# Key maskings of segments 1 to 3 on VectorE or ScalarE instead of GpSimd, and a new order of work, in a memory-attention and gated-FFN kernel

## The chip, the cores and the metric

The kernel runs on one core of a Trainium2 chip. The metric is the device time of one execution in microseconds (us). A core has five engines with an in-order queue each: TensorE (PE, matmuls; its weight loads are shown as PEld), VectorE (DVE), ScalarE (ACT), GpSimd (POOL) and SyncE (SP, which issues most DMAs). They are synchronised by semaphores alone.

## The reference

For 2048 tokens of width 512 (bf16) the reference mixes two branches with a gate per token, `g * a + (1 - g) * b`, g = sigmoid(x . gate_w).

```python
# branch a: 4 segments of 512 tokens, 32 heads of 16 channels
for s in range(4):
    logits = qs @ ks.T * 16 ** -0.5 + causal mask
    a_dot  = softmax(logits) @ vs
    a_mem  = (phi(qs) @ M) / (phi(qs) @ z + 1e-6)      # phi(t) = t + 1 where t > 0, else exp(t)
    out_s  = sigmoid(beta) * a_mem + (1 - sigmoid(beta)) * a_dot
    M += phi(ks).T @ vs;  z += phi(ks).sum()
a = concat(out_s) @ wo
# branch b: F = 1792
b = (relu(x @ W_gate) * (x @ W_up)) @ W_down
```

## The kernel before

The work goes by segments of 512 tokens. For each segment there are: projections q, k, v (`proj`, matmuls at L788 and L786); attention in 18 visits (`att`); the memory part (`mu`, L831, and `nd`, L851 to L863); the FFN in 14 blocks of 128 hidden channels (`ffn`, L1038); and the output (`outp`: L1070 for wo, L1077 for W_down), scaled and evacuated at L1086 and L1087.

Heads are taken in four groups G of eight. Keys lie with channels on partitions, so that 32 partitions hold two heads. The **key masking** (L803 to L807, tile `kp`) makes two copies of each group's 128x512 keys, p = 0 and 1; each copy is multiplied by a per-partition 0/1 column of `pm`, which keeps one head of each pair. So there are 2 x 4 = 8 maskings in a segment, 32 in all. Those of segment 0 run on DVE, the other 24 on POOL. `kp` is a ring of five slots (`kslot`), so a masking waits for the quad group that read its slot last.

A **visit** is a "quad" group of matmuls (L908, 32-row tiles, reading `kp` and `qT`), then an exponential on ACT over 2048 columns (L924, PSUM to `E`), then causal masks of the diagonal blocks on POOL (`affine_select`, L930; one pair of 64- and 128-partition pieces for each diagonal block). When all visits of a head group are through, a **PV** group (L964, 64-row tiles; 16 such groups in all) multiplies the weights with the values, DVE transposes the result (L974), forms and scales the reciprocals (L983, L985), POOL divides (`adT`, L987; in the last segment DVE), and DVE transposes back and adds the memory part (L990 to L993). The phi of two head groups is an ACT exponential (L770) with two DVE pieces: max and add into `ttmp` (L771), minimum (L772). FFN blocks are evacuated by a relu on ACT or DVE (L1046, L1047) and a product on DVE (L1049).

**The order** is not written by hand. Every operation is added to a list with its reads and writes, one or more engines that may run it, and a time for each engine in ns. A list planner (`Sched.run`, `ready`, `_choose`, `place`) plays the five engines forward by those times: it takes the operation that can start first, ties going by the priority of its queue and by a small random jitter, and so fixes each engine's queue and its semaphore waits once and for all. Where an operation names two engines, the planner puts it on the one on which it starts first. The jitter and four further settings (`knob`) are drawn from a list of seeds, one for each 8 us of planned PE time. For an operation whose name stands in `PORT` (key maskings, phi pieces, `rdg`, `ad`, `oa` among them) the planner also books that DVE and POOL wait for each other. On the chip the order is kept and the times are what they are.

The line for the masking before; the ACT form `ka` is defined a line above and not used:

```python
evs.append(sc.add(Op(([("pool", km, 660)] if s else [("dve", km, 350)]), ..., name=f"kmask{s}_{G}_{p}")))
```

Of the kernel before, what the change touches and what calls it, by code (L numbers as in the profile page):

```python
# [9 lines left out]
ALU = mybir.AluOpType  # L10
# [27 lines left out]
ADP = 1  # L38
# [501 lines left out]
def build_kernel(nc, A_x, A_wq, A_wk, A_wv, A_wo, A_beta, W_g, W_u, W_d, gate_w, out):  # L540
    _, S, D = A_x.shape
    F = W_g.shape[1]
    assert D == 512 and S % 512 == 0 and F % 128 == 0
    NSEG, KT, NF, NT = S // 512, D // 128, F // 128, S // 128
    EPS, SCALE = 1e-6, 16 ** -0.5
    sc = Sched(seeds=(140892, 17502, 0, 0, 0, 833601, 583263, 51094, 0, 212245, 56886, 641769, 290654, 823150, 60678, 0, 364216, 4435, 795879, 905041, 409277, 519825, 941044, 25370, 612543, 696634, 0, 758283, 835103, 656834, 0,))
    T = {}
    with contextlib.ExitStack() as stack:
        for name, shape, dt in plan(S, D, F):
            T[name] = stack.enter_context(nc.sbuf_tensor(name, shape, dt))  # L550
        PS = stack.enter_context(nc.psum_tensor("ps", [128, 8, 512], F32))
        for st in sc.streams:
            sc.sem[st] = stack.enter_context(nc.semaphore(f"s_{st}"))
        program(sc, nc, T, PS, A_x, A_wq, A_wk, A_wv, A_wo, A_beta, W_g, W_u, W_d, gate_w, out, NSEG, KT, NF, NT, EPS, SCALE)
        with nc.Block() as block:
            sc.emit(block)
    return sc


def program(sc, nc, T, PS, A_x, A_wq, A_wk, A_wv, A_wo, A_beta, W_g, W_u, W_d, gate_w, out, NSEG, KT, NF, NT, EPS, SCALE):  # L560
# [13 lines left out]
    def dve(fn, occ, **k):  # L574
        return op("dve", fn, occ, **k)
# [190 lines left out]
    def phi(s, px, G, dst, dn, src, slot, rd, acts, sbs):  # L766
        d0 = G - 1 if px == "q" else (G - 1) % EKN
        xv, pv = src[:, slot:slot + 2, :], dst[:, d0:d0 + 2, :]
        wr = [f"{dn}{d0}", f"{dn}{d0 + 1}"]
        acts.append(act(lambda e: e.activation(pv, xv, ACT.Exp), t_act(1024, False), reads=rd, writes=wr, name=f"{px}exp{s}_{G}"))  # L770
        sbs.append((pool if TSP else dve)(lambda e: e.tensor_scalar(V.ttmp[:, :, :], xv, 0.0, 1.0, ALU.max, ALU.add), 1160 if TSP else 400, reads=rd, writes=["ttmp"], name=f"{px}ts{s}_{G}"))  # L771
        sbs.append(dve(lambda e: e.tensor_tensor(pv, pv, V.ttmp[:, :, :], ALU.min), 700, reads=wr + ["ttmp"], writes=wr, name=f"{px}phi{s}_{G}"))  # L772

    def proj(s):
        pes, evs, sbs, acts, sps = [], [], [], [], []
        tok = s % XR * 512

        def pj(w, col, name, wname, tokmajor=False):
            early = s == 0 and name == "q" and col < 3
            ep = Epoch("att" if early else "proj")  # L780
            step = 1 if early else 2
            for k0 in range(0, KT, step):
                def fn(e, k0=k0):
                    for kt in range(k0, k0 + step):
                        if tokmajor:
                            ins = e.matmul(A(ep)[:, :], lhsT=V.xT[:, kt, tok + col * 128:tok + (col + 1) * 128], rhs=w[:, kt, :], start=(kt == 0), stop=(kt == KT - 1))  # L786
                        else:
                            ins = e.matmul(A(ep)[:, :], lhsT=w[:, kt, col * 128:(col + 1) * 128], rhs=V.xT[:, kt, tok:tok + 512], start=(kt == 0), stop=(kt == KT - 1))  # L788
                    return ins
                pes.append(pe(fn, mm(512, step), reads=[f"{wname}{kt}" for kt in range(k0, k0 + step)] + (xt(s) if not early or k0 > 1 else [x for x in xt(s) if x not in ("xT0_3", "xT0_5")]), name=f"{name}{s}_{col}", ep=ep, role="w2" if k0 else "w"))  # L790
            return ep
        def cp(fn, **k):
            return sc.add(Op([("dve", lambda e: fn(e, e.tensor_copy), t_dve(512)), ("act", lambda e: fn(e, lambda d, x: e.activation(d, x, ACT.Copy)), t_act(512))], **k))
        for G in range(4):
            ep = pj(V.wq, G, "q", "wq")
            qs = qslot(s, G)
            evs.append(cp(lambda e, f, ep=ep, qs=qs: f(V.qT[:, qs, :], A(ep)[:, :]), writes=[f"qT{qs}"], name=f"qcp{s}_{G}", ep=ep, role="r"))
            if s > 0 and G % 2:
                phi(s, "q", G, V.phiq, "phiq", V.qT, qs - 1, [f"qT{qs - 1}", f"qT{qs}"], acts, sbs)
            ep = pj(V.wk, G, "k", "wk")  # L800
            evs.append(cp(lambda e, f, ep=ep, G=G: f(V.kT[:, G, :], A(ep)[:, :]), writes=[f"kT{G}"], name=f"kcp{s}_{G}", ep=ep, role="r"))
            ks = kslot(s, G)
            kv = V.kT[:, G, :].rearrange("q (c k) -> q c k", c=8)  # L803
            for p in range(2):
                km = lambda e, kv=kv, p=p, ks=ks: e.tensor_scalar(V.kp[:, ks, :, 64 * p:64 * p + 64], kv, V.pm[:, p:p + 1], None, ALU.mult)  # L805
                ka = lambda e, kv=kv, p=p, ks=ks: e.activation(V.kp[:, ks, :, 64 * p:64 * p + 64], kv, ACT.Copy, scale=V.pm[:, p:p + 1])
                evs.append(sc.add(Op(([("pool", km, 660)] if s else [("dve", km, 350)]), reads=[f"kT{G}", "pm"], writes=[f"kp{ks}_{p}"], name=f"kmask{s}_{G}_{p}")))  # L807
            if s < NSEG - 1 and G % 2:
                phi(s, "k", G, V.ek, "ek", V.kT, G - 1, [f"kT{G - 1}", f"kT{G}"], acts, sbs)
                for g in (G - 1, G):  # L810
                    sps.append(dma("sp", lambda e, g=g: e.dma_start_transpose(V.phik[:, :, g * 128:(g + 1) * 128], V.ek[:, g % EKN, :]), 1 << 17, occ=1280.0, reads=[f"ek{g % EKN}"], writes=[f"phik{g}"], name=f"kT2{s}_{g}"))
        for tt in range(4):
            ep = pj(V.wv, tt, "v", "wv", True)
            evs.append(cp(lambda e, f, ep=ep, tt=tt: f(V.vaug[:, s % 2, tt, :, 0:16], A(ep)[:, :].rearrange("q (h c) -> q h c", c=16)), writes=[f"va{s % 2}_{tt}"], name=f"vcp{s}_{tt}", ep=ep, role="r"))
        if s == 0:
            pes = [p for k in "qkv" for p in pes if p.name[0] == k]
            pes[:3 * KT] = [pes[h * KT + kt] for kt in range(KT) for h in range(3)]
        return pes, evs, sbs, acts, sps
# [25 lines left out]
    def nd(s):  # L844
        pes, ds, sps = [], [], []
        for i in range(4):
# [7 lines left out]
            def nv(ep):  # L854
# [4 lines left out]
            ds.append(dve(lambda e, i=i: e.reciprocal(V.rdm[:, 32 * i:32 * i + 32], V.rdm[:, 32 * i:32 * i + 32]), 345, reads=[f"rdm{i}"], writes=[f"rdm{i}"], name=f"ndr{s}_{i}"))  # L859
            ds.append(dve(lambda e, i=i, ep=ep, rd=rd: e.scalar_tensor_tensor(V.amem[:, i % 2, :].rearrange("q (h c) -> q h c", c=16), nv(ep)[:, :, 0:16], V.gexp[:, 4 * s + i:4 * s + i + 1],  # L860
                                                                             rd.unsqueeze(2).to_broadcast([128, 32, 16]), op0=ALU.mult, op1=ALU.mult),
                          t_dve(512), reads=[f"rdm{i}", f"gexp{s}"], writes=[f"amem{i % 2}"], name=f"ndm{s}_{i}", ep=ep, role="r"))
            sps.append(dma("sp", lambda e, i=i: e.dma_start_transpose(V.amemT[:, :, i * 128:(i + 1) * 128], V.amem[:, i % 2, :]), 1 << 17, occ=1280.0, reads=[f"amem{i % 2}"], writes=[f"amemT{i}"], name=f"aT{s}_{i}"))  # L863
        return pes, ds, sps

# [10 lines left out]
    def att(s, between):  # L876
# [57 lines left out]
        def flush():  # L934
# [47 lines left out]
            gv = V.rdg[:, 32 * (G % (TNN // 2)):32 * (G % (TNN // 2)) + 32].rearrange("q (p c) -> q p c", p=2)  # L982
            ds.append(dve(lambda e: e.reciprocal(rv, Tv[:, :, :, 16]), 345, reads=tn, writes=[f"rden{G % 2}"], name=f"rden{s}_{G}"))  # L983
            ge = V.gexpT[:, 16 * s:16 * s + 16].rearrange("q (a t) -> q t a", t=4).unsqueeze(1).to_broadcast([128, 2, 4, 4])
            ds.append(dve(lambda e: e.tensor_tensor(gv.rearrange("q p (t a) -> q p t a", a=4), rv.rearrange("q p (t a) -> q p t a", a=4), ge, ALU.mult), 215, reads=[f"rden{G % 2}"] + gexpT_r[s], writes=[f"rdg{G % 2}"], name=f"rdg{s}_{G}"))  # L985
            av = V.adT[:, :].rearrange("q (c p e) -> q p c e", p=2, e=16)
            ds.append((dve if s == NSEG - 1 or not ADP else pool)(lambda e: e.tensor_tensor(av, Tv[:, :, :, 0:16], gv.unsqueeze(3).to_broadcast([128, 2, 16, 16]), ALU.mult), 690 if s == NSEG - 1 or not ADP else 1360, reads=tn + [f"rdg{G % 2}"], writes=["adT"], name=f"ad{s}_{G}"))  # L987
            os_ = (s * 4 + G) % OTN
            if s == 0:
                ds.append(dve(lambda e: e.transpose(V.oT[:, os_, :], V.adT[:, :]), t_dve(512), reads=["adT"], writes=[f"oT{os_}"], name=f"bt{s}_{G}"))  # L990
            else:
                ds.append(dve(lambda e: e.transpose(V.oTt[:, :], V.adT[:, :]), t_dve(512), reads=["adT"], writes=["oTt"], name=f"bt{s}_{G}"))
                ds.append(dve(lambda e: e.tensor_tensor(V.oT[:, os_, :], V.oTt[:, :], V.amemT[:, G, :], ALU.add), 435, reads=["oTt"] + [f"amemT{i}" for i in range(4)], writes=[f"oT{os_}"], name=f"oa{s}_{G}"))  # L993
            return pair

        at = {}
# [201 lines left out]
```

## Time and profile before

| | |
|---|---|
| median of 3 runs | 268.11 us (268.04 to 268.27) |
| the profiled execution | 268.02 us, span 266.3 us |
| granted TensorE clock | 1.000 |
| busy: PE, DVE, ACT, POOL | 259.5, 179.1, 176.8, 164.3 us |
| POOL: causal masks L930, key maskings L805, divide L987 | 256 x 435, 24 x 1565, 12 x 1082 ns |
| DVE: L771, L772, L860, L992, L985 | 615, 743, 747, 705, 259 ns (means) |
| ACT: exponentials L924 | 72 x 1875 ns |

The span is the time from the first to the last instruction of the program; the execution holds a little more. A group's line reads: source line, engine, operation, output tile <- input tiles, shapes, count | busy us, mean ns of one | idle time of the engine just before them, and what ended it. A row of the waits reads: who waited <- for whom: us in all, times, longest. A row of the timeline reads: start and length in us, engine, line, operation, count of merged instructions [idle before <- what ended it]; lengths of merged rows include gaps between their instructions. Matmuls are pipelined: one of 512 columns shows 380 ns, while the next starts 216 ns after it, so a busy PE row is read by starts.

### The profile page before, as it was taken

To read this page: it belongs to the slowest core of one execution; us is meant where nothing else is said; L and a number is where in the kernel's file an instruction comes from. 1 tells how busy PE (TensorE), PEld (TensorE's weight loads), DVE (VectorE), ACT (ScalarE), POOL (GpSimd) and SP (SyncE) were. 2 spreads that over 40 slices of the span, in tenths; PEclk is the share of its full clock that TensorE was granted. 3 is DMA by queue.
4 is the path that set the end of the run, shared out by engine and by line. 5 is a ranking of instruction groups with operands and counts; after the bars stand their busy time and mean duration, and the time that the engine had idled before them with its cause. 6 is when DMAs were issued, how large, how long until landed. Compare 5 with 4: busy or idle time off the path is not lost.

```text
span 266.3 us, 6663 instructions
## 1 busy us (share of the span) xinstructions
PE 259.5 (97%) x2748; PEld 113.7 (43%) x2748; DVE 179.1 (67%) x345; ACT 176.8 (66%) x145; POOL 164.3 (62%) x319
## 2 busy tenths in 40 slices
PE   8999999999999898999999999999999999999996
PEld 3434444444344444434444454434443444444444
DVE  5798888866786654299788584766675557567610
ACT  3577899674778655697678766776667577667021
POOL 3016699996689577677648979588655264435200
PEclk9999999999999999999999999999999999999999
DMA  6899249224041032110164013110030121000011
GB/s 187 254 378 204 47 110 335 23 60 76 25 106 23 2 80 60 42 41 4 41 125 102 20 42 81 33 30 0 4 86 0 42 60 42 20 22 0 2 39 39
DMA packets 34527, 19.22 MB, mean 72 GB/s; under 512 B 24001, under 2 KB 33986, under 8 KB 34498
## 3 DMA queue, kind: packets, MB, share of 16 engines
q1 hardware_dynamic: 34368, 18.80, 29.2%
q8 instruction: 21, 0.34, 0.5%
q14 instruction: 8, 0.07, 0.1%
q10 hardware_dynamic: 130, 0.01, 0.0%
HBM read 9.75 MB, written 2.11 MB: 45 GB/s over the span
## 4 chain that ended last, share of the span: by engine, by line
PE 80%; POOL 15%; issue 2%; DVE 2%; ACT 1%; ACTq 0%; POOLq 0%; DVEq 0%
PE ps L1038 32%; PE ps L1077 16%; PE ps L788 9%; PE ps L908 7%; POOL E L930 7%; POOL kp L805 7%; PE ps L964 6%; PE ps L1070 5%; PE ps L786 3%; PE ps L851 1%; PE ps L670 1%; POOL adT L987 1%; ACT E L924 1%; POOL Mbd L840 1%; DVE ek L772 0%
## 5 line engine op out<-in xcount | busy, mean ns | idle before, releaser
L924 ACT ACTIVATE E<-ps 128x2048 bf16<-128x2048 f32 x72 | 135.0, 1875 | 43.8 <-PE ps L908 43.4
L930 POOL TENSOR_SCALAR_AFFINE_SELECT E<-E 64x256 bf16<-64x256 bf16 (+1 forms) x256 | 108.0, 435 | 78.6 <-ACT E L924 64.9
L1038 PE MATMUL ps<-xT,wg 128*128 128x512 bf16 x224 | 59.7, 380 | 0.0
L1038 PE MATMUL ps<-xT,wu 128*128 128x512 bf16 x224 | 58.9, 380 | 0.0
L1077 PE MATMUL ps<-wd,hT 128*128 128x512 bf16 (+2 forms) x238 | 55.1, 367 | 0.0
L1049 DVE TENSOR_TENSOR hT<-ps,rl 128x512 bf16<-128x512 f32 x56 | 38.4, 685 | 18.0 <-PE ps L1038 17.5
L805 POOL TENSOR_SCALAR kp<-kT,pm 128x512 bf16<-128x512 bf16 x24 | 37.5, 1565 | 0.5 <-PE ps L908 0.5
L1077 PEld LDWEIGHTS ps<-wd,hT 128*128 128x128 bf16 x238 | 21.4, 98 | 23.2 <-issue 2.6
L1038 PEld LDWEIGHTS ps<-xT,wg 128*128 128x128 bf16 x224 | 20.2, 98 | 25.6 <-issue 3.6
L974 DVE STREAM_TRANSPOSE Tn<-ps 128x512 f32<-128x512 f32 x32 | 21.2, 694 | 14.6 <-PE ps L964 14.6
L1038 PEld LDWEIGHTS ps<-xT,wu 128*128 128x128 bf16 x224 | 20.1, 98 | 25.4 <-issue 2.5
L908 PE MATMUL ps<-qT,kp 32*128 32x192 bf16 (+7 forms) x512 | 28.6, 287 | 0.0
L1047 DVE TENSOR_SCALAR rl<-ps 128x512 bf16<-128x512 f32 x34 | 23.2, 684 | 2.4 <-PE ps L1038 1.3
L1046 ACT ACTIVATE rl<-ps 128x512 bf16<-128x512 f32 x22 | 13.1, 597 | 13.4 <-PE ps L1038 13.0
L964 PE MATMUL ps<-E,vaug 64*17 64x128 bf16 (+7 forms) x512 | 18.7, 283 | 3.2 <-POOL E L930 3.2
L908 PEld LDWEIGHTS ps<-qT,kp 32*128 32x128 bf16 x512 | 8.2, 92 | 26.2 <-issue 17.8
L1086 DVE TENSOR_SCALAR osb<-ps,omg 128x512 bf16<-128x512 f32 (+1 forms) x8 | 5.5, 688 | 19.5 <-PE ps L1070 10.1
L964 PE MATMUL ps<-E,vsh 64*17 64x128 bf16 (+7 forms) x512 | 18.3, 283 | 0.0
L1087 ACT ACTIVATE osb<-ps,omg 128x512 bf16<-128x512 f32 (+1 forms) x9 | 6.1, 674 | 16.6 <-PE ps L1070 14.4
L964 PEld LDWEIGHTS ps<-E,vaug 64*17 64x17 bf16 x512 | 11.9, 86 | 11.8 <-issue 6.1
L788 PE MATMUL ps<-xT,wq 128*128 128x512 bf16 x64 | 16.4, 379 | 0.3 <-ACT xT L695 0.3
L1070 PE MATMUL ps<-wo,oT 128*128 128x512 bf16 (+2 forms) x68 | 16.5, 367 | 0.0
(74 smaller groups left out, 239.2 us busy)
## 6 DMA issues: line engine op xcount, KB each, us to landing
vsh<-vaug SPq DMA_DIRECT2D x8, 272.0 KB, 3.9
out_dram<-osb SPq DMA_DIRECT2D x15, 128.0 KB, 1.7
wg<-in_B_W_gate_dram SPq DMA_DIRECT2D x8, 224.0 KB, 5.1
wu<-in_B_W_up_dram SPq DMA_DIRECT2D x8, 224.0 KB, 5.3
wd<-in_B_W_down_dram SPq DMA_DIRECT2D x1, 1792.0 KB, 8.9
osb<-in_A_x_dram SPq DMA_DIRECT2D x12, 128.0 KB, 2.1
hT<-in_A_x_dram SPq DMA_DIRECT2D x4, 128.0 KB, 2.2
wq<-in_A_wq_dram SPq DMA_DIRECT2D x4, 128.0 KB, 2.5
```

Of the source, the lines that this page charges most:

```text
L788: ins = e.matmul(A(ep)[:, :], lhsT=w[:, kt, col * 128:(col + 1) * 128], rhs=V.xT[:, kt, tok:tok + 512], start=(kt == 0), stop=(kt == KT - 1))
L805: km = lambda e, kv=kv, p=p, ks=ks: e.tensor_scalar(V.kp[:, ks, :, 64 * p:64 * p + 64], kv, V.pm[:, p:p + 1], None, ALU.mult)
L908: ins = q.matmul(dst, lhsT=V.kp[r, kslot(s, G), c, :], rhs=V.qT[r, qslot(s, G), q0:q0 + w], start=True, stop=True, tile_position=(32 * jj, ...
L924: acts.append(act(lambda a: a.activation(V.E[:, base * 512:base * 512 + min(2048, 4 * W)], PF[:, 0:min(2048, 4 * W)], ACT.Exp, scale=SCALE ...
L930: pools.append(pool(lambda g, ap=ap, lim=lim, pat=pat: g.affine_select(out=ap, in_=ap, compare_op=ALU.is_ge, fill=0.0, base=lim, pattern=[ ...
L964: ins = q.matmul(A(eps[p])[32 * jj:32 * jj + 17, 64 * (c + u):64 * (c + u + n)], lhsT=v[:, 8 * G + 2 * jj + p, :], rhs=V.E[r, f:f + 64 * n ...
L974: ds.append(dve(lambda e, p=p, ep=eps[p]: e.transpose(V.Tn[:, 2 * (G % (TNN // 2)) + p, :], A(ep)[:, :]), t_dve(512), writes=[f"Tn{2 * (G ...
L1038: ins = e.matmul(A(ep)[:, :], lhsT=w[:, kt, f * 128:(f + 1) * 128], rhs=V.xT[:, kt, c % XR * 512:(c % XR + 1) * 512], start=(kt == 0), sto ...
L1047: ("dve", lambda e, ep=eg, r=r: e.tensor_scalar(V.rl[:, r, :], A(ep)[:, :], 0.0, None, ALU.max), t_dve(512))],
L1049: evs.append(dve(lambda e, ep=eu, r=r, hs=hs: e.tensor_tensor(V.hT[:, hs, :], A(ep)[:, :], V.rl[:, r, :], ALU.mult), t_dve(512), reads=[f" ...
L1070: ins = e.matmul(A(ep)[:, 0:c1 - c0], lhsT=V.oT[:, ot[G], i * 128:(i + 1) * 128], rhs=V.wo[:, G, c0:c1], start=st_ and G == 0, stop=sp_ an ...
L1077: ins = e.matmul(A(ep)[:, 0:c1 - c0], lhsT=V.hT[:, slots[f], i * 128:(i + 1) * 128], rhs=V.wd[:, f, c0:c1], start=st_ and f == f0, stop=sp ...
```

## The change

The 24 key maskings of segments 1 to 3 leave POOL. Each may now run on DVE (booked at 380 ns) or on ACT (715 ns), as the planner finds. Eight other figures are changed to new times (that of segment 0's maskings, 350 to 380, among them); in two operations they replace the formula `t_dve(512)` = 688. The list of seeds is another one after its first entry, so that all queues are laid out in another order. The instructions are otherwise the same, in number and shape.

```diff
...
-    sc = Sched(seeds=(140892, 17502, 0, 0, 0, 833601, 583263, 51094, 0, 212245, 56886, 641769, 290654, 823150, 60678, 0, 364216, 4435, 795879, 905041, 409277, 519825, 941044, 25370, 612543, 696634, 0, 758283, 835103, 656834, 0,))
+    sc = Sched(seeds=(140892, 575458, 0, 581332, 635069, 619273, 262375, 763595, 0, 238677, 585783, 19046, 187739, 0, 462444, 519459, 197962, 296149, 243870, 832001, 511906, 535245, 636171, 100007, 0, 121574, 418075, 0, 0, 346384, 0,))
...
-        sbs.append((pool if TSP else dve)(lambda e: e.tensor_scalar(V.ttmp[:, :, :], xv, 0.0, 1.0, ALU.max, ALU.add), 1160 if TSP else 400, reads=rd, writes=["ttmp"], name=f"{px}ts{s}_{G}"))
-        sbs.append(dve(lambda e: e.tensor_tensor(pv, pv, V.ttmp[:, :, :], ALU.min), 700, reads=wr + ["ttmp"], writes=wr, name=f"{px}phi{s}_{G}"))
+        sbs.append((pool if TSP else dve)(lambda e: e.tensor_scalar(V.ttmp[:, :, :], xv, 0.0, 1.0, ALU.max, ALU.add), 1160 if TSP else 590, reads=rd, writes=["ttmp"], name=f"{px}ts{s}_{G}"))
+        sbs.append(dve(lambda e: e.tensor_tensor(pv, pv, V.ttmp[:, :, :], ALU.min), 735, reads=wr + ["ttmp"], writes=wr, name=f"{px}phi{s}_{G}"))
...
-                evs.append(sc.add(Op(([("pool", km, 660)] if s else [("dve", km, 350)]), reads=[f"kT{G}", "pm"], writes=[f"kp{ks}_{p}"], name=f"kmask{s}_{G}_{p}")))
+                evs.append(sc.add(Op(([("dve", km, 380), ("act", ka, 715)] if s else [("dve", km, 380)]), reads=[f"kT{G}", "pm"], writes=[f"kp{ks}_{p}"], name=f"kmask{s}_{G}_{p}")))
...
-                          t_dve(512), reads=[f"rdm{i}", f"gexp{s}"], writes=[f"amem{i % 2}"], name=f"ndm{s}_{i}", ep=ep, role="r"))
+                          745, reads=[f"rdm{i}", f"gexp{s}"], writes=[f"amem{i % 2}"], name=f"ndm{s}_{i}", ep=ep, role="r"))
...
-            ds.append(dve(lambda e: e.tensor_tensor(gv.rearrange("q p (t a) -> q p t a", a=4), rv.rearrange("q p (t a) -> q p t a", a=4), ge, ALU.mult), 215, reads=[f"rden{G % 2}"] + gexpT_r[s], writes=[f"rdg{G % 2}"], name=f"rdg{s}_{G}"))
+            ds.append(dve(lambda e: e.tensor_tensor(gv.rearrange("q p (t a) -> q p t a", a=4), rv.rearrange("q p (t a) -> q p t a", a=4), ge, ALU.mult), 240, reads=[f"rden{G % 2}"] + gexpT_r[s], writes=[f"rdg{G % 2}"], name=f"rdg{s}_{G}"))
-            ds.append((dve if s == NSEG - 1 or not ADP else pool)(lambda e: e.tensor_tensor(av, Tv[:, :, :, 0:16], gv.unsqueeze(3).to_broadcast([128, 2, 16, 16]), ALU.mult), 690 if s == NSEG - 1 or not ADP else 1360, reads=tn + [f"rdg{G % 2}"], writes=["adT"], name=f"ad{s}_{G}"))
+            ds.append((dve if s == NSEG - 1 or not ADP else pool)(lambda e: e.tensor_tensor(av, Tv[:, :, :, 0:16], gv.unsqueeze(3).to_broadcast([128, 2, 16, 16]), ALU.mult), 690 if s == NSEG - 1 or not ADP else 1100, reads=tn + [f"rdg{G % 2}"], writes=["adT"], name=f"ad{s}_{G}"))
-                ds.append(dve(lambda e: e.transpose(V.oT[:, os_, :], V.adT[:, :]), t_dve(512), reads=["adT"], writes=[f"oT{os_}"], name=f"bt{s}_{G}"))
+                ds.append(dve(lambda e: e.transpose(V.oT[:, os_, :], V.adT[:, :]), 705, reads=["adT"], writes=[f"oT{os_}"], name=f"bt{s}_{G}"))
-                ds.append(dve(lambda e: e.transpose(V.oTt[:, :], V.adT[:, :]), t_dve(512), reads=["adT"], writes=["oTt"], name=f"bt{s}_{G}"))
-                ds.append(dve(lambda e: e.tensor_tensor(V.oT[:, os_, :], V.oTt[:, :], V.amemT[:, G, :], ALU.add), 435, reads=["oTt"] + [f"amemT{i}" for i in range(4)], writes=[f"oT{os_}"], name=f"oa{s}_{G}"))
+                ds.append(dve(lambda e: e.transpose(V.oTt[:, :], V.adT[:, :]), 705, reads=["adT"], writes=["oTt"], name=f"bt{s}_{G}"))
+                ds.append(dve(lambda e: e.tensor_tensor(V.oT[:, os_, :], V.oTt[:, :], V.amemT[:, G, :], ALU.add), 470, reads=["oTt"] + [f"amemT{i}" for i in range(4)], writes=[f"oT{os_}"], name=f"oa{s}_{G}"))
```

## The prediction

> **What bounds the kernel now.** I read the page's busy shares first, then the waits of PE, then the key maskings (L805), then POOL's order of work around each wait of PE, and last the load of DVE and ACT where the maskings would go.
>
> ```profile
> span 266.3 us, 6663 instructions
> PE 259.5 (97%) x2748; PEld 113.7 (43%) x2748; DVE 179.1 (67%) x345; ACT 176.8 (66%) x145; POOL 164.3 (62%) x319
> L805 POOL TENSOR_SCALAR kp<-kT,pm 128x512 bf16<-128x512 bf16 x24 | 37.5, 1565 | 0.5 <-PE ps L908 0.5
> ```
>
> PE sets the time: it is the one engine that is nearly always busy. POOL has 38% of the span free on the whole, and 37.5 of its 164.3 us are the 24 key maskings, at 1565 ns each. The waits of PE, all there are:
>
> ```profile
> PE ps L964 <- POOL E L930: 3.2, 5, 1.0
> PE ps L670 <- PEq L1183: 0.8, 1, 0.8
> PE ps L788 <- ACT xT L695: 0.3, 1, 0.3
> ```
>
> The last two belong to the start. In the body PE waits five times, 3.2 us in all, each time at the start of a PV group (L964) for a causal mask on POOL (L930). No row names DVE or ACT after the start. The timeline shows the rest of PE's idle to be cost of changing shape: a quad group of 512 columns starts at 47.38 and the next full matmul at 47.71, 0.33 us where full matmuls follow at 0.216 us; about 0.1 us at each change. 72 quad groups and 16 PV groups make at most 176 changes, 17 us. The reference's work fixes them, and an order can only join a few. POOL ahead of the last of the five waits, and PE's wait itself:
>
> ```profile
> 157.19 2.39 POOL L930 TENSOR_SCALAR_AFFINE_SELECT E<-E 64x256 bf16<-64x256 bf16 x4 [1.14 <-ACT E L924]
> 159.79 0.41 POOL L930 TENSOR_SCALAR_AFFINE_SELECT E<-E 64x256 bf16<-64x256 bf16 x1 [0.21 <-ACT E L924]
> 160.18 1.56 POOL L805 TENSOR_SCALAR kp<-kT,pm 128x512 bf16<-128x512 bf16 x1
> 161.70 0.78 POOL L930 TENSOR_SCALAR_AFFINE_SELECT E<-E 128x256 bf16<-128x256 bf16 x2
> 162.47 1.55 POOL L805 TENSOR_SCALAR kp<-kT,pm 128x512 bf16<-128x512 bf16 x1
> 163.99 0.78 POOL L930 TENSOR_SCALAR_AFFINE_SELECT E<-E 128x256 bf16<-128x256 bf16 x2
> ```
> ```profile
> 164.54 0.39 PE L964 MATMUL ps<-E,vaug 64*17 64x512 bf16 x4 [0.63 <-POOL E L930]
> ```
>
> Two key maskings, 3.1 us, stand between the exponential that ended at 159.7 and the mask that PE waited for. The other four are alike: one masking (42.94) before the 0.21 us at 46.28; two (54.95, 58.52) before the 0.57 us at 61.74; two (84.44, 86.36) before the 1.01 us at 89.76; two (98.53, 100.44) before the 0.79 us at 104.31. The sum is 3.21 us. In the last segment, where no key masking is left after 177.8 us, PE waits for POOL not once. The planner in the kernel, which fixes every queue, books a key masking on POOL at 660 ns; it takes 1556. Each POOL queue thus runs some 0.9 us later than planned per masking, and PE meets its masks too early.
>
> **The change, part by part.**
>
> *Removed from POOL.* 24 x 1.565 = 37.5 us. Taking the maskings out of the queues above moves the awaited mask earlier by 1.56 (46.28) or about 3.1 us (the other four), never past the exponential it needs: the exponentials ended at 59.85 before the wait at 61.74, at 86.26 before 89.76, at 100.34 before 104.31 and at 159.72 before 164.54, each 1.9 us or more ahead with 0.4 to 1.6 us of masks to follow. So all five waits close and the next late thing is PE itself. Gain: 3.2 us. Lower bound 0, if the new order puts other work there; upper bound 3.2 plus about 0.8 from joined groups.
>
> *Added to DVE or ACT.* The same operation stands in the trace for segment 0, on DVE:
>
> ```profile
> L805 POOL TENSOR_SCALAR kp<-kT,pm x24: 1553/1556/1731, 31.5 to 177.8; 128x512 bf16<-128x512 bf16 x24
> L805 DVE TENSOR_SCALAR kp<-kT,pm x8: 341/343/514, 11.7 to 23.4; 128x512 bf16<-128x512 bf16 x8
> ```
>
> On DVE each costs 0.34 us alone. The two at 20.04 and 20.48 took 0.51 and 0.49 because a POOL mask was running with about 0.35 us to go; the others saw none or one about to end. The worst from rows is the masking plus a whole mask, 0.34 + 0.43 = 0.77 us. 24 of them are 8 to 18 us, on DVE's 179: 70 to 74%. ACT has no such row. A bf16 evacuation of 512 columns with a scale per partition (L1087) takes 686 ns, one without (L793) 597, so 0.60 to 0.72 us; I take 0.69, by L1087, which has the scale. All 24 there would be 16.5 us on 177, 73%. In the total there is room either way. The tight stretch is where segment 1's eight maskings were made:
>
> ```profile
> 30.00:60.00 30.00, 29.79 (x364) 12.91 (x363) 24.73 (x43) 25.09 (x21) 27.60 (x41) 1.00 0.54 125
> ```
>
> The columns after PE and PEld are DVE, ACT and POOL: free are 5.3 us on DVE and 4.9 on ACT. Eight maskings need 2.7 to 6.2 us on DVE or 5.5 on ACT; split between them they fit. On the other side, DVE's two phi pieces stretch when POOL runs beside them (L771 426 ns with POOL idle, 872 and 1105 beside L805 maskings), which falls away. What an extra 0.34 us on DVE, or 0.69 on ACT, does to PE depends on slack. For DVE the trace gives no PE wait at all; for ACT, exponentials end 0.56 to 0.78 us before the next quad group in the rows around 40 us, and 0.33 us before it at 157.46. A masking on DVE mostly fits, one on ACT placed just before an exponential costs up to 0.4. As the planner now books both at near the measured price (380 and 715), it will mostly put them where they fit. I take 0.3 us of new small waits in all; 0 to 4 as bounds.
>
> The Trainium skill, "SBUF — State Buffer", section "Summary: rules for kernel authors", speaks against the move: a DVE operation in a two-port mode and a GpSimd one cannot run together, and the later waits for the whole of the earlier. The two stretched rows agree. By that rule 24 maskings could also hold POOL for 24 x 0.34 = 8.2 us, an estimate; that is still less than the 37.5 us that POOL is rid of, so the sum stays.
>
> *A wait that moves.* A masking writes a ring of five slots and must wait for the quad group that last read the slot: 0.33 us at 84.44 and 0.15 at 98.53 on POOL, where only masks queued behind. On DVE the evacuations of projections and FFN queue behind it, and PE waits for those when PSUM banks run out. That is 0.5 us in total in this trace, inside the 0 to 4.
>
> *The other figures and the seeds.* They change no instruction, only the planner's order. The new figures sit near the rows: 745 for L860 (747), 705 for L992 (705), 470 for L993 (489), 240 for L985 (259), 590 and 735 for L771 and L772 (615 and 743 in the mean), 1100 for L987 on POOL (1082). Plan and chip should drift apart less. In price I put it at zero: PE has no gaps left but the waits and changes above. Ten changes of shape more or fewer are 1 us either way.
>
> **Sum.** 266.3 - 3.2 + 0.3 = 263.4 us of span; outside the span lie 268.02 - 266.3 = 1.7 us, so 265.1 for the profiled execution, and 265.2 on the median, which is 0.09 above it. Own range 264.4 to 266.0.
>
> **The rivals.**
> 1. *Half the gain is taken by ACT.* If the planner gives ACT a third of the maskings, eight, and four to five of them delay an exponential past its 0.33 us slack, PE pays 0.36 us each: 1.6 us. For it: ACT idles mostly for PE and its exponentials gate the quads. Against: slack is usually over 0.5. 266.7 us, chance 0.17.
> 2. *No net gain.* The order laid out anew leaves as much in new waits as the old (five PV waits of 0.6). For it: masks cost 435 to 448 ns and are booked at 410. Against: the last segment runs so without a wait. 268.1 us, 0.09.
> 3. *Slower: DVE's queue holds up the evacuations.* Each masking sits in front of an evacuation, takes the stretched 0.51 us beside a POOL mask, and all beyond a slack of 0.33 reaches PE: 24 x 0.18 = 4.3 us, less 3.2 gained: 269.2 us. It decides as soon as 3.2 / 24 = 0.13 us per masking reaches PE. For it: DVE is 82% busy from 30 to 60 us, and it is an in-order queue. Against: no PE wait names DVE, and DVE itself idles 17.5 us waiting for L1038. 0.16.
>
> That the maskings stay on POOL is excluded: the alternatives in the code are DVE and ACT alone.
>
> **How the numbers follow.** Forecast 0.58. A difference of 0.2%, 0.5 us, is about what a measurement of this kernel can tell (its three runs span 268.04 to 268.27). Faster: 0.58 + 0.17 = 0.75; within: 0.09; slower: 0.16. The range runs from 264.0 (some groups joined) to 268.6 and leaves out rival 3 and a few hundredths below.
>
> **What would show it.** Right: no POOL row on L805; PE's waits for L930 gone or under 1 us; POOL near 127 us busy, DVE and ACT together 8 to 17 us more; 24 maskings of 0.34 to 0.51 us (DVE) or 0.6 to 0.72 (ACT). Wrong: PE waits on L908 for ACT's exponentials, or on L1038, L788 and L1077 for DVE evacuations, above 1 us; or PV groups still waiting for masks with POOL half idle. It would also be wrong if the number of shape changes rose by tens.

## The result, and the profile after

The changed kernel takes 264.96 us (264.90 to 265.14, 4 runs), against 268.19 us of the kernel before in the same runs: ratio 0.9875, 95% interval 0.9855 to 0.9895. The profiled execution took 265.14 us, its span 263.4 us. The head of its page:

```profile
span 263.4 us, 6630 instructions
...
PE 255.4 (97%) x2713; PEld 113.6 (43%) x2748; DVE 181.0 (69%) x355; ACT 184.9 (70%) x159; POOL 129.8 (49%) x295
```

POOL is rid of 34.5 us; DVE and ACT carry 10.0 us more together (1.9 and 8.1). PE's count is 35 lower only because this trace lacks the records of 35 matmuls (weight loads are 2748 in both). The waits of PE, all of them:

```profile
PE ps L1038 <- issue: 1.9, 12, 0.2
PE ps L1077 <- issue: 1.0, 6, 0.2
PE ps L670 <- PEq L1183: 0.8, 1, 0.8
PE ps L786 <- issue: 0.6, 4, 0.2
PE ps L788 <- issue: 0.3, 2, 0.2
```

PE's sequencer (PEq) at L670 belongs to the start and was there before. The row `PE ps L964 <- POOL E L930`, 3.2 us before, is gone. The "issue" rows are not waits: each is about 0.2 us, the 216 ns of one matmul whose record is missing. Where the maskings went (line, engine, count, shortest / median / longest in ns, first and last start; then for whom DVE stood idle ahead of them, and who waited for them):

```profile
L805 DVE TENSOR_SCALAR kp<-kT,pm x23: 314/348/1105, 11.4 to 171.7; 128x512 bf16<-128x512 bf16 x23
its engine sat idle before it (us, times) until:
  PE ps L908: 3.9, 3
  ACT kT L793: 1.0, 2
who waited for it (us, times):
  POOL E L930: 5.7, 9
```
```profile
L806 ACT ACTIVATE kp<-kT,pm x9: 712/722/729, 37.8 to 146.1; 128x512 bf16<-128x512 bf16 x9
```

Fifteen of the 24 went to DVE (8 of the 23 are those of segment 0), nine to ACT. The stretch that looked tight, in the order PE, PEld, DVE, ACT, POOL:

```profile
30.00:60.00 30.00, 29.31 (x361) 12.97 (x364) 24.49 (x45) 25.33 (x22) 17.13 (x41) 1.00 0.37 103
```

DVE and ACT are as busy there as before (24.73 and 25.09 us), though maskings were added to both, so the new order must have moved other work out of it. Only POOL fell, from 27.60 to 17.13.

### The profile page after: what moved, and what is told of

Same layout as the page of the kernel before. It is cut to its first block, busy times and chain, and to the rows that moved or that the text cites. A ratio compares the mean times of both kernels' runs of the same rounds, so it can differ in the third digit from the quotient of the medians.

```text
span 263.4 us, 6630 instructions
## 1 busy us (share of the span) xinstructions
PE 255.4 (97%) x2713; PEld 113.6 (43%) x2748; DVE 181.0 (69%) x355; ACT 184.9 (70%) x159; POOL 129.8 (49%) x295
## 4 chain that ended last, share of the span: by engine, by line
PE 94%; DMA 2%; issue 2%; SPq 0%; DVE 0%; DVEq 0%
PE ps L1038 36%; PE ps L1077 19%; PE ps L788 11%; PE ps L908 9%; PE ps L964 7%; PE ps L1070 5%; PE ps L786 5%; DMA phik<-ek 1%; PE ps L851 1%; DMA hT<-in_A_x_dram 1%; PE ps L831 1%; SPq L598 0%; PE ps L683 0%; DVE osb L1086 0%; PE ps L704 0%
## 5 line engine op out<-in xcount | busy, mean ns | idle before, releaser
L930 POOL TENSOR_SCALAR_AFFINE_SELECT E<-E 64x256 bf16<-64x256 bf16 (+1 forms) x256 | 108.9, 437 | 110.1 <-ACT E L924 81.3
L1038 PE MATMUL ps<-xT,wu 128*128 128x512 bf16 x214 | 57.5, 380 | 1.4 <-issue 1.3
L1038 PE MATMUL ps<-xT,wg 128*128 128x512 bf16 x217 | 57.7, 380 | 0.8 <-issue 0.6
L1077 PE MATMUL ps<-wd,hT 128*128 128x512 bf16 (+2 forms) x229 | 52.3, 366 | 1.1 <-issue 1.0
L1047 DVE TENSOR_SCALAR rl<-ps 128x512 bf16<-128x512 f32 x31 | 21.3, 688 | 5.0 <-PE ps L1038 4.3
L1046 ACT ACTIVATE rl<-ps 128x512 bf16<-128x512 f32 x25 | 14.9, 598 | 12.8 <-PE ps L1038 12.8
L964 PE MATMUL ps<-E,vaug 64*17 64x128 bf16 (+7 forms) x512 | 18.7, 283 | 0.0
L964 PE MATMUL ps<-E,vsh 64*17 64x128 bf16 (+7 forms) x512 | 18.3, 283 | 0.0
L788 PE MATMUL ps<-xT,wk 128*128 128x512 bf16 x62 | 16.2, 380 | 0.2 <-issue 0.2
L786 PE MATMUL ps<-wv,xT 128*128 128x512 bf16 x59 | 15.1, 380 | 0.7 <-issue 0.6
```

The source lines that it names most:

```text
L930: pools.append(pool(lambda g, ap=ap, lim=lim, pat=pat: g.affine_select(out=ap, in_=ap, compare_op=ALU.is_ge, fill=0.0, base=lim, pattern=[ ...
L964: ins = q.matmul(A(eps[p])[32 * jj:32 * jj + 17, 64 * (c + u):64 * (c + u + n)], lhsT=v[:, 8 * G + 2 * jj + p, :], rhs=V.E[r, f:f + 64 * n ...
L1038: ins = e.matmul(A(ep)[:, :], lhsT=w[:, kt, f * 128:(f + 1) * 128], rhs=V.xT[:, kt, c % XR * 512:(c % XR + 1) * 512], start=(kt == 0), sto ...
L1047: ("dve", lambda e, ep=eg, r=r: e.tensor_scalar(V.rl[:, r, :], A(ep)[:, :], 0.0, None, ALU.max), t_dve(512))],
L1077: ins = e.matmul(A(ep)[:, 0:c1 - c0], lhsT=V.hT[:, slots[f], i * 128:(i + 1) * 128], rhs=V.wd[:, f, c0:c1], start=st_ and f == f0, stop=sp ...
```

## The experiments

Three explanations were to be told apart. **A**: POOL carried more time than its plan booked, ran late, and PE met its masks too early; within it, **A1** says that the load on POOL is the cost and **A2** that the error of the plan is. **B**: the new order and seeds give the gain. **D**: the other measured figures give it. "Seeds searched anew" below means that seeds were drawn at random and kept where the planner's own end came earlier; the chip's times played no part in it.

**1. The old order, with less work on POOL.**

```diff
+kn = ... e.tensor_scalar(V.kp[:, ks, 0:2, 64 * p:64 * p + 64], kv[:, 0:2, :], V.pm[:, p:p + 1], None, ALU.mult)
+# and once, at the start: e.memset(V.kp[:, 4, :, :], 0.0)
-[("pool", km, 660)] if s else [("dve", km, 350)]
+[("pool", kn, 660)] if s else [("dve", km, 350)]
```

Each masking on POOL covers only two of the eight blocks of keys; the other columns of the copy keep what stood there.

> The kernel before, every queue and every wait as it was, but each of the 24 POOL maskings writes only 2 of the 8 key blocks (a quarter of its columns; the rest of the keys is left unmasked or stale), so its time on POOL falls from 1565 ns to an estimated 0.5 us. Theory A (the whole gain is POOL's load taken away ahead of the causal masks): PE's five waits for L930 close, span 263.1, median 264.9, ratio 0.988. Rival B (the gain is the new order with the measured figures): nothing moves, median 268.1, ratio 1.000.

Measured: 265.06 us, ratio 0.9868 (0.9852 to 0.9885). Span 263.7. No PE wait for a mask is left. The groups of POOL (L806 is the masking in this kernel, L931 the masks):

```profile
L931 POOL TENSOR_SCALAR_AFFINE_SELECT E<-E 64x256 bf16<-64x256 bf16 (+1 forms) x256 | 106.7, 429 | 96.5 <-ACT E L925 78.4 <-DVE ek L772 3.1 <-DVE ttmp L771 2.3
L806 POOL TENSOR_SCALAR kp<-kT,pm 128x128 bf16<-128x128 bf16 x24 | 15.2, 633 | 2.0 <-DVE kT L801 0.9 <-PE ps L909 0.9
```

At 633 ns the masking takes what the plan had booked for it, 660, and with the order as it was (one clearing of 0.95 us at the start is added) the whole gain is there. That is A against B: no new order is needed for the gain. It does not tell A1 from A2, as the edit takes both the load and the error away.

**2. The same for segment 2 alone.**

```diff
-[("pool", km, 660)] if s else [("dve", km, 350)]
+[("pool", kn if s == 2 else km, 660)] if s else [("dve", km, 350)]
```

> The kernel before, queues and waits as they were, with only the 8 maskings of segment 2 cut to a quarter of their columns (about 0.6 us each as in narrow_pool; the other keys of that segment stay unmasked or stale). Their places are ahead of the waits at 89.76 and 104.31. Theory A: those two waits close, 1.01 + 0.79 = 1.8 us, the other three, 1.4 us, stay: span 264.5 to 264.9, ratio 0.992 to 0.994. Rival E (the five waits are one lag that POOL carries along, so that closing two changes the others as well): gain of under 1 us or over 2.5.

Measured: 266.23 us, ratio 0.9923 (0.9911 to 0.9936), a gain of 2.1 us; span 264.9.

```profile
PE ps L965 <- POOL E L931: 1.2, 2, 0.6
```

Two of five waits are left, of 0.6 us each. Those of 1.01 and 0.79 us closed as expected, and the gain lies between the two limits set for rival E: each of the four larger waits belongs to the maskings just ahead of it. The one of 0.21 us at 46.28 does not show either, though segment 2's maskings come after it. Two small shifts in this execution account for it: PE was ready for that group at 46.80 us, against 46.07 before (46.28 less the wait), about 0.7 us later, 0.4 of them from longer waits at the start; the mask that it needs ended at 46.59 in place of 46.14, only 0.45 us later, as a pause of POOL of 0.49 us behind a DVE phi piece (L771) did not occur.

**3. The masking line alone.** The seeds stay, but the planner lays out another order, as DVE and ACT now hold other work.

```diff
-[("pool", km, 660)] if s else [("dve", km, 350)]
+[("dve", km, 380), ("act", ka, 715)] if s else [("dve", km, 380)]
```

> The kernel before with the masking line alone changed: 24 maskings on DVE or ACT, the old seeds and the old figures, so the planner lays out another order from seeds that were picked for the old one. Theory A, if taking load off POOL is enough in any order: 264.9 to 266, ratio 0.988 to 0.992. Rival B (the order is half of the change): slower than that, 268 or more, with PE idle somewhere that no POOL wait explains.

Measured: 268.86 us, ratio 1.0018 (1.0009 to 1.0027): nothing gained, as rival B had it for this run. POOL's waits are gone, and others stand in their place (the profiled execution was the longest of the ten, 269.69 us):

```profile
PE ps L964 <- DVE rdm L859: 1.1, 1, 1.1
PE ps L1077 <- issue: 1.1, 7, 0.2
PE ps L670 <- PEq L1183: 0.8, 1, 0.8
PE ps L908 <- ACT E L924: 0.5, 2, 0.3
PE ps L1070 <- DVE rdm L858: 0.4, 1, 0.4
```

PE's list does not show all of it: between the groups of matmuls there are more gaps of 0.1 to 0.6 us, many of them from 110 to 140 and at 200 to 203 us, most behind DVE evacuations and ACT exponentials. So the masking line does not give the gain in every order.

**4. The masking line alone, seeds searched anew** (the edit of 3 and other seeds).

> The kernel before with the masking line changed and a list of seeds of its own, searched anew for this kernel by the planner's own end; all other figures are the old ones. Theory A with order (POOL must be rid of the maskings and the order must be fitted to it, the other figures don't matter): 264.5 to 265.7, ratio 0.986 to 0.991. Rival D (the measured figures of the vector pieces are needed for a good order): 266.5 or more.

Measured: 265.87 us, ratio 0.9907 (0.9894 to 0.9920). It lies between the two bands that were written down, nearer to A's (up to 265.7). Its span is 263.6 us, with one wait of 0.6 us for a weight's DMA (`wq`) at the start. With an order searched for them, the old figures of the vector pieces cost about 0.9 us against the changed kernel (265.87 - 264.96, not run side by side, and with other seeds), and not the 3 us that D would have.

**5. The changed kernel with the old seeds.**

```diff
-seeds=(140892, 575458, 0, 581332, ...)
+seeds=(140892, 17502, 0, 0, ...)
```

> The changed kernel with the seeds of the kernel before: maskings on DVE or ACT, the new figures, yet another order. Theory A: no PE wait for L930, 264.5 to 266, ratio 0.987 to 0.992. Rival B (these seeds are needed): 267 or more.

Measured: 265.18 us, ratio 0.9877 (0.9862 to 0.9892), as good as the changed kernel. The new seeds as such are not what the gain came from. Runs 3 and 5 were measured side by side and differ in the eight figures alone: with the old seeds these were worth 3.7 us (268.86 - 265.18). So the line needs either seeds searched for it (run 4) or figures near the chip's times (this run). Whether such figures make most orders good, or these seeds gave a good one by luck, one order cannot tell.

**6. All of the change but the masking line, seeds searched anew.**

```diff
-[("dve", km, 380), ("act", ka, 715)] if s else [("dve", km, 380)]
+[("pool", km, 660)] if s else [("dve", km, 380)]
```

> The changed kernel with the maskings back on POOL at the old 660 ns, the other new figures kept, and seeds searched anew. Theory A: PE waits for L930 are back at 2 to 4 us, median 267 to 269, ratio 0.996 to 1.003. Rival D (the other measured figures give the gain): 266 or less.

Measured: 270.71 us, ratio 1.0080 (1.0060 to 1.0100), slower than the kernel before and than expected. Three of its six executions had a granted clock of 0.994 and took 271.0 to 271.3 us; the other three, at 1.000, took 269.4 to 270.4, which is slower than before as well.

```profile
PE ps L964 <- POOL E L930: 4.5, 4, 2.3
```

The measured figures and a searched order gain nothing while the masking is booked at 660 and takes 1556 ns or more (1607 in the mean here). D, as an explanation by itself, falls.

**7. The maskings on POOL, booked at what they take, seeds searched anew.**

```diff
-[("pool", km, 660)] if s else [("dve", km, 350)]
+[("pool", km, 1560)] if s else [("dve", km, 350)]
```

> The kernel before with the 24 maskings still on POOL, but booked at 1560 ns in place of 660, and seeds searched anew for it. Theory A1 (POOL's load itself is the cost): the masks come late whatever the plan says, PE waits for L930 stay at 1.5 us or more, 266.5 to 268.5. Theory A2 (the error of the plan was the cost, not the engine): the plan keeps PE clear of late masks, waits for L930 under 0.7 us, 264.8 to 266, ratio 0.988 to 0.992.

Measured: 265.31 us, ratio 0.9886 (0.9874 to 0.9899); span 263.4, that of the changed kernel.

```profile
PE 254.8 (97%) x2713; PEld 113.0 (43%) x2748; DVE 177.4 (67%) x345; ACT 176.5 (67%) x145; POOL 160.1 (61%) x319
```
```profile
L805 POOL TENSOR_SCALAR kp<-kT,pm x24: 1555/1556/1569, 30.3 to 174.5; 128x512 bf16<-128x512 bf16 x24
```

POOL is as loaded as before (160.1 us against 164.3), each masking takes its 1556 ns, and PE waits for no mask. A2 holds against A1: at the same load, in an order laid out by the right price, nothing is lost, and moving the work to engines whose price was right was one way to mend the plan's error. This order is a new one too; run 6, also searched anew but with the price at 660 (and with the other new figures), is its control. Each of the two is one search, so how far such orders scatter is not known.

**8 and 9. The changed order, with POOL time given back.** The first causal mask of the visits next to which the old kernel had maskings is made wider to the right, where it keeps every element.

```diff
+k = 64 + (min(128 * EXTRA.get(vid, 0), 64 * (parts[0][3] - 1)) if i == 0 else 0)   # 256 in place of 128 in the second
-[W, 4]] + dims + [[1, 64]])        pattern=[[0, 4]] + pat + [[1, 64]]
+[W, 4]] + dims + [[1, k]])         pattern=[[0, 4]] + pat + [[1, k]]
```

> The changed kernel, every queue and wait as it is, but POOL gets back what it lost: in the 19 visits next to which the old order had key maskings on POOL, the first causal mask covers 128 to 256 columns more (they are kept as they are, so the output stays), some 24 x 1.6 us of unbooked POOL time. Theory A: PE waits for L930 come back; as this plan books nothing for that load where the old one booked 660 ns for each, at least as much as before, 3 to 6 us, median 268 to 271, ratio 1.00 to 1.01. Rival B (the new order gives the gain): stays near 265, ratio 0.988 to 0.992.

> The same edit as the wide masks with twice the extra columns where the row of columns has room (the output stays): by the 0.86 ns a column that wide_masks showed (877 ns for 768 columns, 440 for 256), 33 us of unbooked POOL time, against 20 us there; the maskings on POOL cost the old kernel 37.5 us, of which its plan booked 15.8. Theory A: PE's waits for L930 grow much faster than the load, from 0.7 us to 2 to 5 us, median 267 to 270, ratio 0.995 to 1.006. Rival C (the new order has so much slack that POOL's load no longer counts): 266 or less, ratio 0.992 or less.

Measured: 265.87 us, ratio 0.9905 (0.9890 to 0.9920), and 270.57 us, ratio 1.0082 (1.0068 to 1.0097). First the smaller, then the larger dose:

```profile
PE ps L966 <- POOL E L932: 0.7, 2, 0.4
```
```profile
PE ps L966 <- POOL E L932: 4.7, 3, 1.9
```
```profile
L932 POOL TENSOR_SCALAR_AFFINE_SELECT E<-E 64x256 bf16<-64x256 bf16 (+5 forms) x256 | 143.1, 573 | 84.3 <-ACT E L925 63.3 <-DVE kp L805 3.8 <-DVE ek L772 3.5
```

The masks take 108.9 us in the changed kernel, 130.2 in the first of these and 143.1 in the second: 21 and 34 us that no plan knows of. The first missed theory A's band (268 to 271) and lies in the one written down for rival B. My expectation was too high twice over: a wider mask costs less than I had assumed, and the new order swallows most of 21 us. To that extent B has a point: this order bears lateness on POOL better than the old one did. The second is 0.6 us past the upper end of theory A's band. In one table, with PE's waits for masks beside the POOL time that the plan did not book for maskings or widened masks (before: 24 x (1565 - 660) = 21.7 us). The causal masks themselves, booked at 410 ns and taking 435, add some 6 us in every kernel and are left out:

| kernel | unbooked on POOL, us | PE's waits for masks, us |
|---|---|---|
| 1, narrow maskings, old order | -0.6 | 0 |
| 7, POOL at its real price | 0 | 0 |
| changed kernel | 0 | 0 |
| 8, first dose | 21 | 0.7 |
| before | 21.7 | 3.2 |
| 6, all but the masking line | 22.7 | 4.5 |
| 9, second dose | 34 | 4.7 |

An order has some slack, and lateness beyond it reaches PE: from the first dose to the second, 13 us more on POOL cost 4.0 us more of PE's waits. How much slack there is differs from order to order: 21 to 23 us cost 0.7, 3.2 and 4.5 us.

**10 and 11. One engine alone,** each with seeds searched anew.

```diff
-[("dve", km, 380), ("act", ka, 715)] if s else [("dve", km, 380)]
+[("act", ka, 715)] if s else [("dve", km, 380)]      # act_only_s
+[("dve", km, 380)]                                   # dve_only_s
```

> The changed kernel with ACT alone for the 24 maskings, seeds searched anew by the planner's own end. My rival 1 of the prediction: maskings of 0.71 us delay exponentials past their slack, 1 us or more of PE waits for ACT, 266.5 or more. Theory A (whatever engine is booked at its real time serves): PE waits for ACT under 0.5 us, 264.8 to 265.9, ratio 0.987 to 0.992.

> The changed kernel with DVE alone for the 24 maskings, seeds searched anew. My rival 3 of the prediction: maskings wait in DVE's queue for slots and masks, the evacuations behind them are late, 1 us or more of PE waits for DVE, 266.5 or more. Theory A: 264.8 to 265.9, ratio 0.987 to 0.992.

Measured: ACT alone 265.35 us, ratio 0.9889 (0.9876 to 0.9903), with no PE wait for ACT. DVE alone 267.12 us, ratio 0.9956 (0.9942 to 0.9970), past the line that I had drawn for rival 3, but by another cause:

```profile
PE ps L1038 <- DMA wg<-in_B_W_gate_dram: 1.7, 2, 1.2
...
PE ps L1038 <- DVE kp L805: 0.2, 1, 0.2
```

This order starts the FFN before its weights have landed; 1.7 of the 2.2 us by which it is slower than the changed kernel (267.12 - 264.96, not run side by side) are two waits for that DMA. Waits for a masking on DVE are 0.2 us. Rival 3's mechanism isn't shown by it, and whether a better order exists with DVE alone was not tried.

## Why the prediction was right, point by point

- *All five PV waits close, 3.2 us.* They did. Run 1 shows that the maskings were the cause of all five, and run 2 that two of the larger ones belong to the maskings just ahead of them.
- *0.3 us of new small waits.* The size came out by luck, the place did not. No PE wait for DVE or ACT appeared in the body; but in the profiled execution the first projection starts at 5.88 us in place of 5.34, as the transposes at the start (L683) wait longer for the tokens' DMA. That is start-up, which the change doesn't touch: the same wait, 0.4 us, shows in run 1 with the old order. The span was forecast at 263.4 and is 263.4; of the 3.2 us that closed, 0.54 went at the start, and some 0.2 came from elsewhere.
- *Cost of a masking.* DVE 348 ns in the median (0.34 said), ACT 722 (0.69 taken, upper bound 0.72). The upper bound of 0.77 us on DVE was too low: the longest took 1105 ns, as the bound was made with a mask on POOL and not with the longer divide (1082 ns). The slack covered it.
- *The tight stretch.* "Split between them they fit" was right in the result and wrong in the picture: the new order left DVE and ACT at the old load there.
- *The slot wait in DVE's queue.* It came, larger than on POOL (3.9 us in 3 places against 0.5), and reached PE in none of them.
- *Seeds and figures at zero.* This was the weak step. Run 3, with the masking line but without new seeds or figures, loses all of the gain; with either the new seeds (run 4) or the new figures (run 5) it has most or all of it. So the two are not worth nothing: one of them at least is needed, and "plan and chip should drift apart less" was the right idea with no price put on it. A rival that the order alone can eat the gain, by waits for DVE and ACT, was missing. The nearest, rival 2, had nearly that time (268.1, run 3 measured 268.86) and another cause.
- *Rivals 1 and 3* don't occur in the searched orders (runs 10 and 11); in run 3, waits of both kinds do.
- *The reason.* The prediction named both POOL's load and the plan's error of 0.9 us per masking, and put the gain down to the load. Run 7 shows the same gain with the load left where it was and the error mended. In that the forecast was lucky: the change took away the load and the error in one step, so both readings gave the same number.

## What to carry to other kernels

Where a planner fixes the order, compare each booked time with the trace before moving any work: an operation that takes 1556 ns and is booked at 660 delays all that is queued behind it, and PE pays wherever the order's slack runs out, though the engine is idle 38% of the time. A right price and an order searched with it on the old engine were worth as much as two new engines. When one line changes what the planner sees, do not judge the line by one order: with the old figures the same line was worth nothing with the old seeds and 2.5 us with new ones, and with the new figures the old seeds served as well.

## What the runs showed of the hardware

- On POOL the masking, a multiply by a per-partition scalar, costs (1556 - 602) / 384 = 2.5 ns for each further column (medians at 512 and 128 columns), the causal select only (877 - 440) / 512 = 0.85 ns (means at 768 and 256). The planner's formula for POOL, 160 ns and 0.975 ns a column, was near for the select (410 ns for 256 columns); for the masking it gives the 660 ns that were booked, and the chip took 2.4 times that.
- A masking on DVE took 1105 ns at 157.47 us, beside a POOL divide (L987) that had 957 ns to go; with no POOL operation beside it, 314 to 354 ns. POOL's rows there:

```profile
157.37 1.06 POOL L987 TENSOR_TENSOR adT<-Tn,rdg 128x512 bf16<-128x512 f32 x1 [0.76 <-DVE rdg L985]
158.71 3.17 POOL L930 TENSOR_SCALAR_AFFINE_SELECT E<-E 64x256 bf16<-64x256 bf16 x6 [0.28 <-DVE kp L805]
```

  In turn, the mask at 158.71 started 0.13 us after the end of that masking, though the last exponential had ended at 157.79. The Trainium skill ("SBUF — State Buffer", "Who interferes with whom") says that DVE in its two-port mode and GpSimd take a shared pair of ports for a whole instruction. These rows agree, in both directions. Not every pair in the traces does: in the kernel before, L771 on DVE took 652 ns from 35.48 us, wholly within a masking on POOL that ran from 35.00 to 36.73 us, against 426 ns with POOL idle.
- The prediction estimated that DVE maskings could hold POOL for 8.2 us. The row `POOL E L930: 5.7, 9` counts all the idle time that ended with a DVE masking, and two of its nine places belong to segment 0. Only 3.2 us of it lie after the masking had begun, 2.6 us of them beside the maskings that were moved; what held POOL in the other 2.5 us is not shown.
